# A fused attention and FFN kernel: casting loads on the GpSimd queue and a head pinned on TensorE

## The chip, the cores and the metric

The kernel runs on one core of a Trainium2 chip. The metric is the device time of one execution in microseconds (us). A run is called slow when its time is more than 1.5% above the fastest of the same kernel; such runs are left out of every comparison.

## The reference

Sliding-window causal attention is followed by a feed-forward network (FFN) with a squared ReLU, everything given and returned in fp32.

```python
# q, k, v: (8, 8, 576, 64)   batch, heads, tokens, head dimension
rel = pos[:, None] - pos[None, :]
mask = (rel >= 0) & (rel < 64)                      # window of 64
attn = softmax(where(mask, scale * q @ k.T, -1e9))
x = (attn @ v).transpose(0, 2, 1, 3).reshape(4608, 512)
h = maximum(x @ w_in, 0)                            # w_in  512 x 2048
out = (h * h) @ w_out                               # w_out 2048 x 512
```

The 4608 tokens are processed as 36 chunks of 128 tokens. Four chunks make one group of 512 for the FFN.

## The kernel before

All loads go out on the sync queue as fp32. DVE casts `w_in`, and GpSimd (POOL) casts `w_out`, q, k and v to fp16. Within a chunk each 64-token block attends to itself and to the block before it, so the values are kept twice: `v_ev` holds the chunk's own 128 rows, and `v_od` holds the same rows moved by 64. The lower half of `v_od` comes from the previous chunk. Both are rings of eight buffers.

```python
NV = 8
v_evs = [const.tile([P, H, 66], FP16, name=f"v_ev{i}") for i in range(NV)]
v_ods = [const.tile([P, H, 66], FP16, name=f"v_od{i}") for i in range(NV)]

def load(i):
    # ... k, q, v to fp32 staging tiles on the sync queue; GpSimd casts k and q ...
    v_ev, v_od, v_next = v_evs[i % NV], v_ods[i % NV], v_ods[(i + 1) % NV]
    nc.gpsimd.tensor_copy(out=v_ev[:, :, 0:D], in_=sts[2][:])
    nc.gpsimd.tensor_copy(out=v_od[64:P, :, 0:D], in_=v_ev[0:64, :, 0:D])
    if i + 1 < NCK:
        nc.gpsimd.tensor_copy(out=v_next[0:64, :, 0:D], in_=v_ev[64:P, :, 0:D])

def values(i):
    # ... for each head h and both 64-token blocks blk ...
    vv = (v_ods if blk == 0 else v_evs)[i % NV]
    nc.tensor.matmul(av[64 * blk:64 * blk + 64, h % 4, 0:65],
                     pms[i][h % 2][:, h // 2, blk, :], vv[:, h, 0:65], start=True, stop=True)
```

The head of the program treats the first eight chunks singly. T transposes q and k, S_ makes the scores, V multiplies by the values, and X transposes the result for the FFN. The `warm(n)` calls are matmuls without use that keep the clock of TensorE (PE) up. Below is the program order. The framework's scheduler may reorder it, but it respects every dependency that program order creates through a buffer.

```python
load(0)
for s in load_w_in(): s()
for i in range(1, NV - 1):
    load(i)
T(0), warm(6), S_(0), warm(6), V(0), warm(6), X(0), warm(4)
load(NV - 1)                       # chunk 7 is loaded AFTER V(0)
for s in load_w_out() + ffn_up_chunk(0): s()
T(1), S_(1), warm(2), V(1), T(2), warm(2), X(1), S_(2)
for i in range(1, NFIRST):
    up = ffn_up_chunk(i)
    up[0](), V(i + 1), T(i + 2), up[1](), up[2](), X(i + 1), S_(i + 2), up[3]()
# ... then groups: ffn_out(g-1), ffn_up(g), attention(g+1), loads(g+2), woven ...
```

The softmax here doesn't subtract the row's maximum and nothing guards it: scores larger than these inputs give would overflow.

## Time and profile before

| | before |
|---|---|
| median (4 runs) | 347.35 us (346.05 to 348.84) |
| profiled span | 345.9 us |
| PE busy | 324.3 us |

The page of the profile gives each engine's busy time. Below that are rows of 40 digits, each the busy share of one slice of 8.65 us in tenths. PEclk is the granted PE clock in tenths of full speed, and DMA is the mean busy share of the 16 DMA engines.

```profile
PE 324.3 (94%) x3146; PEld 178.2 (52%) x3146; DVE 207.9 (60%) x506; ACT 163.8 (47%) x289; POOL 121.5 (35%) x204
...
PE   1957888999999999999999999999999999999995
...
DVE  2656988852666776676776657665675566544400
...
PEclk9996999999999999999999999999999999999998
DMA  7799987899972455546877757730011000000021
```

PE is full from about the ninth slice on, so PE work bounds the kernel there. What can be gained lies in the first 75 us, and that is also where the DMA engines are near full. The table by stage of the same kernel gives, for each stretch, its length, the busy us of each engine (with instruction counts), the clock, the DMA share and GB/s.

```profile
core 0: us, PE busy (x) PEld busy (x) DVE busy (x) ACT busy (x) POOL busy (x), PEclk, DMA share, GB/s
0.00:20.00 20.00, 11.39 (x85) 5.24 (x86) 9.29 (x44) 2.97 (x4) 4.83 (x15) 1.00 0.76 222
20.00:75.00 55.00, 46.39 (x813) 40.10 (x811) 42.93 (x98) 29.01 (x52) 38.22 (x63) 0.94 0.94 240
75.00:100.00 25.00, 25.00 (x269) 13.71 (x267) 12.88 (x40) 10.28 (x19) 19.65 (x32) 1.00 0.89 214
100.00:346.00 246.00, 241.54 (x1989) 119.18 (x1987) 142.77 (x325) 121.51 (x215) 58.85 (x95) 1.00 0.37 96
```

From 20 to 75 us PE is busy 46.4 of 55 us, and DVE 42.9. After 75 us PE has no idle except the tail. Two more lines are wanted later. The first, from the timeline, is the first matmul of V(0), with its start and duration in us:

```profile
15.17 0.22 PE L211 MATMUL av<-v_od_121,pm_327 128*64 128x65 f16 x1 [0.26 <-DVE pm_327 L201]
```

The second is from the DMA issues of the first 8 us. It is the load of chunk 0's v, with its size and the us from issue to landing:

```profile
v_st<-in_v_dram SPq DMA_DIRECT2D x1, 256.0 KB, 3.9
```

V(0) starts at 15.2 us and waits only for its mask step on DVE.

### The profile page before, as it was taken

How to read it: one execution, taken by the hardware profiler on the slowest of the kernel's cores; microseconds unless marked ns; L12 is line 12 of the kernel's file. 1: busy time of each engine (PE TensorE's matmuls, PEld its weight loads, DVE VectorE, ACT ScalarE, POOL GpSimd, SP SyncE). 2: the span in 40 equal slices, each digit the busy share in tenths (PEclk: the TensorE clock that was granted, in tenths of full speed). 3: DMA queues.
4: the chain of work that ended last, by engine and by line, in shares of the span. 5: the costliest groups of instructions: out<-in, count | busy, mean ns of one | idle time of the engine just before them, and what ended most of it. 6: DMA issues, size and time to landing. Idle time of an engine off the chain costs nothing.

```text
span 345.9 us, 7917 instructions
## 1 busy us (share of the span) xinstructions
PE 324.3 (94%) x3146; PEld 178.2 (52%) x3146; DVE 207.9 (60%) x506; ACT 163.8 (47%) x289; POOL 121.5 (35%) x204
## 2 busy tenths in 40 slices
PE   1957888999999999999999999999999999999995
PEld 0346787875555555445545554455445544544442
DVE  2656988852666776676776657665675566544400
ACT  1123457544535646643664466436544654444411
POOL 4009895497753333316566544530000000000000
PEclk9996999999999999999999999999999999999998
DMA  7799987899972455546877757730011000000021
GB/s 200 249 252 239 234 247 252 207 230 228 243 172 61 93 121 123 121 124 155 212 185 182 170 135 184 185 87 27 23 45 36 30 32 32 30 30 32 35 88 62
DMA packets 122341, 46.65 MB, mean 135 GB/s; under 512 B 113600, under 2 KB 113600, under 8 KB 122304
## 3 DMA queue, kind: packets, MB, share of 16 engines
q1 hardware_dynamic: 122304, 46.15, 51.7%
q8 instruction: 24, 0.39, 0.5%
q14 instruction: 13, 0.11, 0.1%
HBM read 36.70 MB, written 9.44 MB: 133 GB/s over the span
## 4 chain that ended last, share of the span: by engine, by line
PE 83%; DVE 7%; DMA 5%; ACT 2%; SPq 1%; issue 1%; ACTq 0%
PE ops L296 37%; PE hps L250 28%; DMA ws<-in_moe_w_in_dram 5%; PE qkT_ps L173 4%; PE av L211 4%; PE xt_ps L224 2%; DVE h_397 L276 1%; DVE h_1087 L276 1%; DVE xT L226 1%; DVE w_in_sb L117 1%; PE hps_639 L271 1%; SPq L151 1%; SPq L115 0%; PE hps_1088 L271 0%; PE hps_1537 L271 0%
## 5 line engine op out<-in xcount | busy, mean ns | idle before, releaser
L250 PE MATMUL hps<-xT,w_in_sb 128*128 128x512 f16 x448 | 115.2, 379 | 0.0
L254 ACT ACTIVATE hrelu<-hps 128x512 f32<-128x512 f32 x112 | 66.8, 598 | 91.6 <-PE hps L250 90.9
L250 PEld LDWEIGHTS <-w_in_sb 128*128 128x128 f16 x448 | 43.7, 98 | 52.6 <-issue 0.3
L271 PEld LDWEIGHTS <-w_in_sb 128*128 128x128 f16 x512 | 31.2, 99 | 8.2 <-issue 3.9
L301 ACT ACTIVATE osb<-ops 128x512 f32<-128x512 f32 x36 | 21.6, 600 | 29.1 <-PE ops L296 28.9
L182 ACT ACTIVATE qT<-qkT_ps 128x512 f16<-128x512 f16 x36 | 21.5, 596 | 22.6 <-DVE kT L180 22.3
L216 DVE TENSOR_TENSOR x_sb<-av,rden 128x256 f16<-128x256 f32 x72 | 27.5, 415 | 0.1
L180 DVE COPY kT<-qkT_ps 128x512 f16<-128x512 f16 x36 | 15.2, 421 | 18.0 <-PE qkT_ps L173 17.8
L226 DVE COPY xT<-xt_ps 128x512 f16<-128x512 f16 x36 | 15.1, 420 | 12.7 <-PE xt_ps L224 12.7
L215 DVE RECIPROCAL rden<-av 128x4 f32<-128x4 f32 x72 | 11.4, 178 | 17.1 <-PE av L211 17.1
L255 DVE SCALAR_TENSOR_TENSOR h_5222<-hps,hrelu 128x512 f16<-128x512 f32 x16 | 11.1, 691 | 16.6 <-ACT hrelu L254 16.6
L296 PE MATMUL ops<-w_out_sb,h_1087 128*128 128x512 f16 x64 | 17.5, 380 | 0.0
L191 PEld LDWEIGHTS <-kT 64*128 64x128 f16 x576 | 11.0, 95 | 12.2 <-issue 9.6
L296 PE MATMUL ops<-w_out_sb,h_3120 128*128 128x512 f16 x64 | 16.5, 380 | 0.0
L296 PE MATMUL ops<-w_out_sb,h_2579 128*128 128x512 f16 x64 | 16.5, 380 | 0.0
L296 PE MATMUL ops<-w_out_sb,h_4199 128*128 128x512 f16 x64 | 16.5, 380 | 0.0
L296 PE MATMUL ops<-w_out_sb,h_3658 128*128 128x512 f16 x64 | 16.5, 380 | 0.0
L296 PE MATMUL ops<-w_out_sb,h_2041 128*128 128x512 f16 x64 | 16.5, 380 | 0.0
L296 PE MATMUL ops<-w_out_sb,h_4736 128*128 128x512 f16 x64 | 16.4, 379 | 0.0
L296 PE MATMUL ops<-w_out_sb,h_397 128*128 128x512 f16 x64 | 15.3, 380 | 0.0
L224 PE MATMUL xt_ps<-ident,x_sb 128*128 128x128 f16 x144 | 15.1, 222 | 0.1
L255 DVE SCALAR_TENSOR_TENSOR h_4736<-hps,hrelu 128x512 f16<-128x512 f32 x16 | 11.0, 689 | 6.8 <-ACT hrelu L254 6.4
(837 smaller groups left out, 611.1 us busy)
## 6 DMA issues: line engine op xcount, KB each, us to landing
out_dram<-osb SPq DMA_DIRECT2D x36, 256.0 KB, 2.2
k_st<-in_k_dram SPq DMA_DIRECT2D x32, 256.0 KB, 3.9
q_st<-in_q_dram SPq DMA_DIRECT2D x32, 256.0 KB, 4.0
v_st<-in_v_dram SPq DMA_DIRECT2D x32, 256.0 KB, 4.1
ws<-in_moe_w_in_dram SPq DMA_DIRECT2D x16, 256.0 KB, 4.2
k_st<-in_k_dram SPq DMA_DIRECT2D x8, 128.0 KB, 3.2
q_st<-in_q_dram SPq DMA_DIRECT2D x8, 128.0 KB, 3.0
v_st<-in_v_dram SPq DMA_DIRECT2D x8, 128.0 KB, 3.2
```

What stands on the lines that cost most here:

```text
L173: nc.tensor.transpose(out=ps[:, s, hp, :], in_=src[i][:, hp * P:(hp + 1) * P], identity=ident[:])
L180: nc.vector.tensor_copy(out=kT[:, :, 64:192], in_=ps[:, 0])
L182: nc.scalar.activation(out=qT[:], in_=ps[:, 1], func=AF.Copy, scale=1.0)
L216: nc.vector.tensor_tensor(out=x_sb[:, 4 * half:4 * half + 4, :], in0=av[:, :, 0:D], in1=rden[:].to_broadcast([P, 4, D]), op=ALU.mult)
L224: nc.tensor.transpose(out=xt[:, c, :], in_=xs[i][:, 2 * c:2 * c + 2, :], identity=ident[:])
L226: nc.vector.tensor_copy(out=xT_of(i // 4)[:, :, (i % 4) * P:(i % 4 + 1) * P], in_=xt[:])
L250: nc.tensor.matmul(hps[:], w_in_sb[:, c, f * P:(f + 1) * P], xT_of(g)[:, c, :], start=(c == 0), stop=(c == DMC - 1))
L254: nc.scalar.activation(out=hrelu[:], in_=hps[:], func=AF.Relu)
L255: nc.vector.scalar_tensor_tensor(out=h2s[g][:, f, :], in0=hps[:], scalar=0.0, in1=hrelu[:], op0=ALU.max, op1=ALU.mult)
L271: nc.tensor.matmul(hps[:, f, :], w_in_sb[:, c, (4 * fq + f) * P:(4 * fq + f + 1) * P], xT_of(g)[:, c, t0:t0 + P], start=(c == 0), stop=(c ...
L296: nc.tensor.matmul(hold["ps"][:], h2s[g][:, f, ts * P:(ts + 1) * P], w_out_sb[:, f, :], start=(f == 0), stop=(f == FFC - 1))
L301: nc.scalar.activation(out=osb[:], in_=hold["ps"][:], func=AF.Copy, scale=OUT_SCALE)
```

## The change

The intent is to free DVE and POOL from casts and to feed PE earlier. Every load but chunk 0's becomes a casting transfer on the GpSimd queue, straight to fp16. The weights come in quarters of 1 MB (read) placed between the chunks. The shifted copies of v become transfers from SBUF to SBUF on the sync queue. PE's order for the first eight chunks is written out by hand, chunk by quarter of the FFN, and pinned. Cut to its core:

```diff
+    def shift_v(i):
+        v_ev, v_od, v_next = v_evs[i % NV], v_ods[i % NV], v_ods[(i + 1) % NV]
+        nc.sync.dma_start(out=v_od[64:P, :, 0:D], in_=v_ev[0:64, :, 0:D])
+        if i + 1 < NCK:
+            nc.sync.dma_start(out=v_next[0:64, :, 0:D], in_=v_ev[64:P, :, 0:D])
+
+    def load(i):
+        # ... for k, q, v:
+                nc.gpsimd.dma_start(out=dst[p0:p1, :, 0:D], in_=src[b, :, t0:t0 + p1 - p0, :]...)
+        shift_v(i)
+    # load_first(): chunk 0 as before in fp32 on the sync queue, cast on DVE and ACT
+    # load_w_in(quar), load_w_out(quar): one casting gpsimd transfer each
...
+    load_first()
+    load_w_in(0)
+    load_w_in(1)
     # ... masks ...
-    load(0)
-    for s in load_w_in():
-        s()
-    for i in range(1, NV - 1):
+    load(1)
+    load_w_in(2)
+    load(2)
+    load_w_in(3)
+    for i in range(3, NV):
         load(i)
-    T(0), warm(6), S_(0), warm(6), V(0), warm(6), X(0), warm(4)
-    load(NV - 1)
-    for s in load_w_out() + ffn_up_chunk(0):
-        s()
-    T(1), S_(1), warm(2), V(1), T(2), warm(2), X(1), S_(2)
-    for i in range(1, NFIRST):
-        ...
+    for quar in range(4):
+        load_w_out(quar)
+    with tc.manual_schedule(engines={mybir.EngineType.PE}):
+        T(0), warm(4), S_(0), warm(4), V(0), warm(4), X(0), warm(2)
+        up_chunk(0, 0), warm(4), up_chunk(0, 1), warm(4)
+        T(1), S_(1), warm(2), V(1), warm(2), X(1), up_chunk(1, 0)
+        up_chunk(0, 2), up_chunk(1, 1), up_chunk(1, 2), T(2), S_(2), up_chunk(0, 3), V(2)
+        up_chunk(1, 3), X(2), T(3), up_chunk(2, 0), S_(3), up_chunk(2, 1)
+        for i in range(2, NFIRST):
+            # V(i+1), up(i,2), X(i+1), T(i+2), up(i,3), S_(i+2), up(i+1,0), up(i+1,1)
```

More of the change, by code (lines that the diff above doesn't have):

```diff
@@ L45 @@
     NB = S // 64
-    W_SCALE = 100.0
-    OUT_SCALE = 1.0 / (W_SCALE * W_SCALE)
+    H_SCALE = 1.0e4
+    OUT_SCALE = 1.0 / H_SCALE
     BIG = 65504.0
@@ L53 @@
     const = ctx.enter_context(tc.tile_pool(name="const", bufs=1))
-    wst = ctx.enter_context(tc.tile_pool(name="wst", bufs=4))
-    stage = ctx.enter_context(tc.tile_pool(name="stage", bufs=15))
+    stage = ctx.enter_context(tc.tile_pool(name="stage", bufs=3))
     st16 = ctx.enter_context(tc.tile_pool(name="st16", bufs=8))
@@ L65 @@
     ps_att = ctx.enter_context(tc.tile_pool(name="ps_att", bufs=4, space=bass.MemoryType.PSUM))
+    NV = 8
+    FQ = DFF // 4
+    NFIRST = 8
     ident = const.tile([P, P], FP16, name="ident")
+    base = const.tile([P, 64], FP16, name="base")
+    w_in_q = [const.tile([P, DMC, FQ], FP16, name=f"w_in{i}") for i in range(4)]
+    w_out_q = [const.tile([P, 4, DM], FP16, name=f"w_out{i}") for i in range(4)]
+    v_evs = [const.tile([P, H, 66], FP16, name=f"v_ev{i}") for i in range(NV)]
+    v_ods = [const.tile([P, H, 66], FP16, name=f"v_od{i}") for i in range(NV)]
@@ new lines, with pieces @@
+    k16s, q16s = {}, {}
+    def pieces(i):
+        b0, j0 = divmod(2 * i, NB)
+        if j0 + 1 < NB:
+            return [(0, P, b0, 64 * j0)]
+        return [(0, 64, b0, 64 * j0), (64, P, b0 + 1, 0)]
+    def shift_v(i):
[4 more added lines that the diff above has]
+    def load(i):
+        k16s[i] = st16.tile([P, H, D], FP16, name="k16", tag="k16")
+        q16s[i] = st16.tile([P, H, D], FP16, name="q16", tag="q16")
+        for (src, dst) in ((k, k16s[i]), (q, q16s[i]), (v, v_evs[i % NV])):
+            for (p0, p1, b, t0) in pieces(i):
+                nc.gpsimd.dma_start(
+                    out=dst[p0:p1, :, 0:D],
+                    in_=src[b, :, t0:t0 + p1 - p0, :].rearrange("h p d -> p h d"))
+        shift_v(i)
@@ new lines, in load_first @@
+    def load_first():
+        k16s[0] = st16.tile([P, H, D], FP16, name="k16", tag="k16")
+        q16s[0] = st16.tile([P, H, D], FP16, name="q16", tag="q16")
+        for (src, dst, cast) in ((k, k16s[0], nc.vector.tensor_copy),
+                                 (q, q16s[0], nc.scalar.copy),
+                                 (v, v_evs[0], nc.vector.tensor_copy)):
+            st = stage.tile([P, H, D], FP32, name="first_st", tag="st")
+            nc.sync.dma_start(out=st[:], in_=src[0, :, 0:P, :].rearrange("h p d -> p h d"))
+            cast(out=dst[:, :, 0:D], in_=st[:])
+        shift_v(0)
@@ new lines, in load_w_in, with load_w_out @@
+    def load_w_in(quar):
+        nc.gpsimd.dma_start(
+            out=w_in_q[quar][:],
+            in_=moe_w_in[:, quar * FQ:(quar + 1) * FQ].rearrange("(c p) n -> p c n", p=P))
+    def load_w_out(quar):
+        nc.gpsimd.dma_start(
+            out=w_out_q[quar][:],
+            in_=moe_w_out[4 * quar * P:4 * (quar + 1) * P, :].rearrange("(f p) n -> p f n", p=P))
+    for i in range(NV):
+        nc.vector.memset(v_evs[i][:, :, 64:65], 1.0)
+        nc.vector.memset(v_ods[i][:, :, 64:65], 1.0)
@@ L68 @@
+    nc.vector.memset(v_ods[0][0:64, :, 0:D], 0.0)
     make_identity(nc, ident[:])
-    base = const.tile([P, 64], FP16, name="base")
+    load_first()
+    load_w_in(0)
+    load_w_in(1)
     nc.gpsimd.memset(base[:], BIG)
@@ L96 @@
     mask_second = make_mask("mask_second", 1)
-    w_in_sb = const.tile([P, DMC, DFF], FP16, name="w_in_sb")
-    w_out_sb = const.tile([P, FFC, DM], FP16, name="w_out_sb")
-    NV = 8
-    v_evs = [const.tile([P, H, 66], FP16, name=f"v_ev{i}") for i in range(NV)]
-    v_ods = [const.tile([P, H, 66], FP16, name=f"v_od{i}") for i in range(NV)]
-    for i in range(NV):
-        nc.vector.memset(v_evs[i][:, :, 64:65], 1.0)
-        nc.vector.memset(v_ods[i][:, :, 64:65], 1.0)
-    nc.vector.memset(v_ods[0][0:64, :, 0:D], 0.0)
-    def load_w_in():
-        steps = []
-        FQ = DFF // 4
-        def one(quar, c):
-            ws = wst.tile([P, FQ], FP32, name="ws", tag="ws")
-            nc.sync.dma_start(out=ws[:], in_=moe_w_in[c * P:(c + 1) * P,
-                                                      quar * FQ:(quar + 1) * FQ])
-            nc.vector.tensor_scalar(
-                out=w_in_sb[:, c, quar * FQ:(quar + 1) * FQ], in0=ws[:],
-                scalar1=W_SCALE, scalar2=None, op0=ALU.mult)
-        for quar in range(4):
-            for c in range(DMC):
-                steps.append(lambda quar=quar, c=c: one(quar, c))
-        return steps
-    def load_w_out():
-        def one(f):
-            ws = wst.tile([P, DM], FP32, name="ws2", tag="ws")
-            nc.sync.dma_start(out=ws[:], in_=moe_w_out[f * P:(f + 1) * P, :])
-            nc.gpsimd.tensor_copy(out=w_out_sb[:, f, :], in_=ws[:])
-        return [lambda f=f: one(f) for f in range(FFC)]
     xTs = {}
@@ L140, in xT_of @@
         return xTs[g]
-    q16s, k16s, qTs, kTs, pms, xs = {}, {}, {}, {}, {}, {}
-    def load(i):
-        sts = []
-        for (src, nm) in ((k, "k"), (q, "q"), (v, "v")):
-            st = stage.tile([P, H, D], FP32, name=f"{nm}_st", tag="st")
-            b0, j0 = divmod(2 * i, NB)
-            if j0 + 1 < NB:
-                nc.sync.dma_start(
-                    out=st[:], in_=src[b0, :, 64 * j0:64 * j0 + P, :].rearrange("h p d -> p h d"))
-            else:
-                nc.sync.dma_start(
-                    out=st[0:64], in_=src[b0, :, 64 * j0:S, :].rearrange("h p d -> p h d"))
-                nc.sync.dma_start(
-                    out=st[64:P], in_=src[b0 + 1, :, 0:64, :].rearrange("h p d -> p h d"))
-            sts.append(st)
-        k16s[i] = st16.tile([P, H * D], FP16, name="k16", tag="k16")
-        nc.gpsimd.tensor_copy(out=k16s[i][:], in_=sts[0][:].rearrange("p h d -> p (h d)"))
-        q16s[i] = st16.tile([P, H * D], FP16, name="q16", tag="q16")
-        nc.gpsimd.tensor_copy(out=q16s[i][:], in_=sts[1][:].rearrange("p h d -> p (h d)"))
-        v_ev, v_od, v_next = v_evs[i % NV], v_ods[i % NV], v_ods[(i + 1) % NV]
-        nc.gpsimd.tensor_copy(out=v_ev[:, :, 0:D], in_=sts[2][:])
-        nc.gpsimd.tensor_copy(out=v_od[64:P, :, 0:D], in_=v_ev[0:64, :, 0:D])
-        if i + 1 < NCK:
-            nc.gpsimd.tensor_copy(out=v_next[0:64, :, 0:D], in_=v_ev[64:P, :, 0:D])
+    qTs, kTs, pms, xs = {}, {}, {}, {}
     def transposes(i):
@@ L172, in transposes @@
             for hp in range(HP):
-                nc.tensor.transpose(out=ps[:, s, hp, :], in_=src[i][:, hp * P:(hp + 1) * P],
+                nc.tensor.transpose(out=ps[:, s, hp, :], in_=src[i][:, 2 * hp:2 * hp + 2, :],
                                     identity=ident[:])
@@ L242, with h2_of, square @@
     h2s = {}
+    def h2_of(g):
+        if g not in h2s:
+            h2s[g] = h2pool.tile([P, FFC, 512], FP16, name="h2", tag="h2")
+        return h2s[g]
+    def square(out, hps, hrelu):
+        nc.scalar.activation(out=hrelu, in_=hps, func=AF.Relu, scale=H_SCALE)
+        nc.vector.scalar_tensor_tensor(
+            out=out, in0=hps, scalar=0.0, in1=hrelu, op0=ALU.max, op1=ALU.mult)
     def ffn_up(g):
-        h2s[g] = h2pool.tile([P, FFC, 512], FP16, name="h2", tag="h2")
         def one(f):
@@ L250, in one, with up_chunk @@
                 nc.tensor.matmul(
-                    hps[:], w_in_sb[:, c, f * P:(f + 1) * P], xT_of(g)[:, c, :],
+                    hps[:], w_in_q[f // 4][:, c, f % 4 * P:(f % 4 + 1) * P], xT_of(g)[:, c, :],
                     start=(c == 0), stop=(c == DMC - 1))
             hrelu = hrp.tile([P, 512], FP32, name="hrelu", tag="hrelu")
-            nc.scalar.activation(out=hrelu[:], in_=hps[:], func=AF.Relu)
-            nc.vector.scalar_tensor_tensor(
-                out=h2s[g][:, f, :], in0=hps[:], scalar=0.0, in1=hrelu[:],
-                op0=ALU.max, op1=ALU.mult)
+            square(h2_of(g)[:, f, :], hps[:], hrelu[:])
         return [lambda f=f: one(f) for f in range(FFC)]
-    def ffn_up_chunk(i):
+    def up_chunk(i, fq):
         g, t0 = i // 4, i % 4 * P
-        if g not in h2s:
-            h2s[g] = h2pool.tile([P, FFC, 512], FP16, name="h2", tag="h2")
-        def one(fq):
-            hps = ps_up.tile([P, 4, P], FP32, name="hps4", tag="ps_u")
-            for f in range(4):
-                for c in range(DMC):
-                    nc.tensor.matmul(
-                        hps[:, f, :], w_in_sb[:, c, (4 * fq + f) * P:(4 * fq + f + 1) * P],
-                        xT_of(g)[:, c, t0:t0 + P], start=(c == 0), stop=(c == DMC - 1))
-            hrelu = hrp.tile([P, 4, P], FP32, name="hrelu4", tag="hrelu")
-            nc.scalar.activation(out=hrelu[:], in_=hps[:], func=AF.Relu)
-            nc.vector.scalar_tensor_tensor(
-                out=h2s[g][:, 4 * fq:4 * fq + 4, t0:t0 + P], in0=hps[:], scalar=0.0,
-                in1=hrelu[:], op0=ALU.max, op1=ALU.mult)
-        return [lambda fq=fq: one(fq) for fq in range(FFC // 4)]
+        hps = ps_up.tile([P, 4, P], FP32, name="hps4", tag="ps_u")
+        for f in range(4):
+            for c in range(DMC):
+                nc.tensor.matmul(
+                    hps[:, f, :], w_in_q[fq][:, c, f * P:(f + 1) * P],
+                    xT_of(g)[:, c, t0:t0 + P], start=(c == 0), stop=(c == DMC - 1))
+        hrelu = hrp.tile([P, 4, P], FP32, name="hrelu4", tag="hrelu")
+        square(h2_of(g)[:, 4 * fq:4 * fq + 4, t0:t0 + P], hps[:], hrelu[:])
     def warm(n):
@@ L294, in one @@
                 hold["ps"] = ps_out.tile([P, DM], FP32, name="ops", tag="ps_o")
-            for f in range(4 * fq, 4 * fq + 4):
+            for f in range(4):
                 nc.tensor.matmul(
-                    hold["ps"][:], h2s[g][:, f, ts * P:(ts + 1) * P], w_out_sb[:, f, :],
-                    start=(f == 0), stop=(f == FFC - 1))
+                    hold["ps"][:], h2s[g][:, 4 * fq + f, ts * P:(ts + 1) * P], w_out_q[fq][:, f, :],
+                    start=(fq == 0 and f == 0), stop=(fq == 3 and f == 3))
             if fq == 3:
@@ L306, in ffn_out @@
         return [lambda ts=ts, fq=fq: one(ts, fq) for ts in range(4) for fq in range(4)]
-    load(0)
-    for s in load_w_in():
-        s()
-    NFIRST = 8
-    for i in range(1, NV - 1):
-        load(i)
-    T, S_, V, X = [lambda i, fn=fn: fn(i) if i < NFIRST else None
-                   for fn in (transposes, scores, values, to_xT)]
-    T(0), warm(6), S_(0), warm(6), V(0), warm(6), X(0), warm(4)
-    load(NV - 1)
-    for s in load_w_out() + ffn_up_chunk(0):
-        s()
-    T(1), S_(1), warm(2), V(1), T(2), warm(2), X(1), S_(2)
-    for i in range(1, NFIRST):
-        up = ffn_up_chunk(i)
-        up[0](), V(i + 1), T(i + 2), up[1](), up[2](), X(i + 1), S_(i + 2), up[3]()
+    load(1)
[3 more added lines that the diff above has]
+    for i in range(3, NV):
+        load(i)
+    for quar in range(4):
+        load_w_out(quar)
+    with tc.manual_schedule(engines={mybir.EngineType.PE}):
+        T, S_, V, X = transposes, scores, values, to_xT
+        T(0), warm(4), S_(0), warm(4), V(0), warm(4), X(0), warm(2)
[4 more added lines that the diff above has]
+        for i in range(2, NFIRST):
+            steps = [lambda: V(i + 1), lambda: up_chunk(i, 2), lambda: X(i + 1),
+                     lambda: T(i + 2), lambda: up_chunk(i, 3), lambda: S_(i + 2),
+                     lambda: up_chunk(i + 1, 0), lambda: up_chunk(i + 1, 1)]
+            live = [i + 1 < NFIRST, True, i + 1 < NFIRST, i + 2 < NFIRST, True,
+                    i + 2 < NFIRST, i + 1 < NFIRST, i + 1 < NFIRST]
+            for step, on in zip(steps, live):
+                if on:
+                    step()
     for s in loads(2):
```

## The prediction

> **What bounds the kernel now.** TensorE. The page has PE busy 324.3 of 345.9 us. From 86.5 us to its end at about 341.6 us the table by stage shows no idle. The matmul counts confirm it: FFN matmuls of 512 columns stream at 0.213 us, 16 of 128 columns at 0.9 us, one chunk's attention at about 1.75 us. All of the program's useful matmuls then sum to about 310 us (448 up + 576 out x 0.213, 512 small up x 0.056, 36 x 1.75), an estimate. So 310 us are PE work, 4.3 tail, some 31 lost in the first 70 us. There the DMA engines are 70 to 106% busy at 200 to 270 GB/s (table of slices), DVE is at 83 to 96% between 34 and 69 us, and the granted clock falls to 0.5 between 26 and 32 us.
>
> **What the change removes and adds.** Removed: 16 weight casts on DVE (0.43 us each, 7 us) and every POOL cast (0.61 us each, 121.5 us busy in all). POOL was never the bound, so that is worth nothing after 70 us. DVE relief is worth a few us in the head. Added: three descriptor-generating DMAs per chunk on POOL, and two SBUF-to-SBUF shifts per chunk on the sync queue. The matmul count is unchanged. If PE ran its new head unhindered from about 20 us, the kernel would end near 335 us.
>
> **Why I expect no such gain.** The compiled instruction order shows that pinning the eight chunks does not keep other matmuls out: the scheduler has put first output-projection matmuls, which need the first and second quarter of w_out, before chunk 1's last transposes and before chunk 1's first up-projection. PE runs in order, so it stops there, with only about 5.5 us of useful work done, until two w_out quarters have landed. On the load queue these are behind all of w_in and chunks 1 to 7: 12.6 MB in all.
> The bytes are unchanged, and in the head the DMA engines are already near full. The Trainium skill, "DMA: Bandwidth & Descriptors", section "Issuing engines are not separate DMA queues", says that transfers run on the same 16 engines whichever engine starts them; so I expect no more bandwidth from the GpSimd queue. Estimates from this trace: 256 KB of q, k or v per 1.1 us (19 in 22.5 us), so 23.5 us for seven chunks; weights at about 350 GB/s (366 GB/s at 12 to 14 us), 18 us for 6 MB; chunk 0 and start 6 us; shifts 3 to 4 us. The second w_out quarter lands at about 51 us.
> After that PE is fed: 51 + 304.5 of remaining work + 4.3 tail + 2.5 for a cold clock after the stall = 362 us.
>
> **Prediction:** 362 us, 8 in 10 between 350 and 388. Faster by over 2%: 0.06; within 2%: 0.14; slower by over 2%: 0.80.
>
> **What would show it.** Right: a PE gap of 20 to 35 us ending at 45 to 60 us, released by a w_out transfer, ahead of a two-matmul output group; the clock at 0.5 around its end; PE full afterwards; DVE free of weight casts; DMA near full until the gap ends. Wrong: PE busy through 20 to 50 us, or gaps released by chunk loads or DVE.
>
> **What would make it wrong.** Casting transfers moving faster than the 240 GB/s seen here (w_out by 35 us would make it even, below that faster). Descriptor generation on POOL slower than about 1.1 us per 256 KB transfer: the stall grows one for one, and above about 2.5 us the loads would bound the later stages too, giving 390 us or more.

## The result

| | before | after |
|---|---|---|
| median | 347.35 us (346.05 to 348.84, 4 runs) | 380.74 us (379.83 to 381.78, 4 runs) |
| profiled span | 345.9 us | 378.0 us |
| PE busy | 324.3 us | 322.9 us |
| ratio to before, 95% interval | 1 | 1.0956 (1.0919 to 1.0993) |

A ratio, here and below, is the one that the record gives for the fast runs of two kernels measured in the same rounds, with its 95% interval. It isn't quite the ratio of the medians quoted. The change makes the kernel 33.4 us slower. The prediction was slower by 14.6.

The page of the profile after:

```profile
PE 322.9 (85%) x3146; PEld 177.4 (47%) x3146; DVE 196.3 (52%) x492; ACT 164.6 (44%) x290; POOL 105.5 (28%) x134
...
PE   1400047999999999999999999999999999999996
...
DVE  1300014477878765756665665666566665744310
...
PEclk9965558999999999999999999999999999999999
DMA  8999995599999999799779959996110000001012
```

There is a hole in PE from the third to the fifth slice, with the clock down to half. From the eighth slice PE is full. The table by stage of the kernel after, first two stretches:

```profile
0.00:20.00 20.00, 5.44 (x32) 2.08 (x32) 4.69 (x29) 3.58 (x5) 13.54 (x24) 1.00 1.37 162
20.00:75.00 55.00, 20.15 (x233) 13.55 (x233) 9.62 (x23) 6.82 (x12) 20.97 (x26) 0.66 1.31 121
```

In the 55 us from 20 to 75, PE does 20.2 us of work against 46.4 before. That one stretch loses 26.2 us, and the first 20 us lose 6.0, together 32.2. PE's busy time as a whole is nearly unchanged and the spans differ by 32.1, so the whole loss is in the head. (DMA shares above 1 mean that packets overlap on an engine.)

What PE waited for, from the view of waits (columns: engine, tile and line, releaser, then total us, times, longest us):

```profile
PE av L207 <- DMA v_od<-v_ev: 33.9, 1, 33.9
PE warm L279 <- DVE mask_inner L145: 8.7, 1, 8.7
PE qkT_ps L169 <- DVE k L111: 4.6, 1, 4.6
```

One wait of 33.9 us stands out. The prediction named a `w_out` transfer as its releaser, and "gaps released by chunk loads or DVE" as the sign of being wrong. The releaser is part of a chunk load: the shift of the values, `v_od<-v_ev`. The timeline shows where it ends:

```profile
52.77 0.21 PE L207 MATMUL av<-v_od,pm 128*64 128x65 f16 x1 [33.88 <-DMA v_od<-v_ev]
```

This is the first matmul of V(0), which had started at 15.2 us before. The chain of waits from 34 us to there (start, us, what ran):

```profile
33.87 0.81 POOL q L97
34.68 6.81 DMA v_ev<-in_v_dram
...
41.50 0.59 SPq L87
...
42.15 10.58 DMA v_od<-v_ev
52.73 0.04 issue
52.77 0.65 PE av L207 x13
```

The transfer at 34.68 us is the v of chunk **7**. When it lands, the sync queue issues chunk 7's shift, which takes 10.58 us, and only then does PE start the values of chunk **0**. Two lines of the DMA issues tell how busy the engines were (the first v of chunk 0 on the sync queue, and the four `w_out` quarters; size written and median us to landing):

```profile
first_st<-in_v_dram SPq DMA_DIRECT2D x1, 256.0 KB, 11.2
...
w_out<-in_moe_w_out_dram POOLq DMA_DIRECT2D x4, 512.0 KB, 11.3
```

### The profile page after: what moved, and what is told of

Same layout as the page of the kernel before. It is cut to its first block, busy times and chain, and to the rows that moved or that the text cites. A ratio compares the mean times of both kernels' runs of the same rounds, so it can differ in the third digit from the quotient of the medians.

```text
span 378.0 us, 7791 instructions
## 1 busy us (share of the span) xinstructions
PE 322.9 (85%) x3146; PEld 177.4 (47%) x3146; DVE 196.3 (52%) x492; ACT 164.6 (44%) x290; POOL 105.5 (28%) x134
## 3 DMA queue, kind: packets, MB, share of 16 engines
HBM read 36.70 MB, written 9.44 MB: 122 GB/s over the span
## 4 chain that ended last, share of the span: by engine, by line
PE 76%; DMA 10%; ACT 5%; DVE 4%; POOL 3%; issue 1%; SPq 0%; ACTq 0%; POOLq 0%
PE ops L289 33%; PE hps L255 26%; DMA w_in<-in_moe_w_in_dram 6%; PE hps L269 5%; PE av L207 4%; PE qkT_ps L169 3%; PE sc L187 3%; DMA v_od<-v_ev 3%; ACT hrelu L246 3%; DVE h L247 2%; PE xt_ps L220 2%; DMA v_ev<-in_v_dram 2%; ACT pm L195 1%; PE warm L279 1%; POOL v_ev L97 1%
## 5 line engine op out<-in xcount | busy, mean ns | idle before, releaser
L289 PE MATMUL ops<-w_out,h 128*128 128x512 f16 x576 | 149.9, 382 | 0.0
L247 DVE SCALAR_TENSOR_TENSOR h<-hps,hrelu 128x512 f16<-128x512 f32 x144 | 99.3, 690 | 65.5 <-ACT hrelu L246 63.0
L255 PE MATMUL hps<-xT,w_in 128*128 128x512 f16 x448 | 115.0, 379 | 0.0
L289 PEld LDWEIGHTS <-h 128*128 128x128 f16 x576 | 49.7, 98 | 41.9 <-issue 0.6
L255 PEld LDWEIGHTS <-w_in 128*128 128x128 f16 x448 | 43.8, 98 | 52.9
L97 POOL DMA_DIRECT2D v_ev<-in_v_dram x39 | 32.8, 841 | 90.1 <-PE av L207 86.1
L97 POOL DMA_DIRECT2D k<-in_k_dram x39 | 33.0, 847 | 58.5 <-PE qkT_ps L169 55.9
L207 PE MATMUL av<-v_od,pm 128*64 128x65 f16 x288 | 17.6, 200 | 35.0 <-DMA v_od<-v_ev 33.9
L195 ACT ACTIVATE pm<-sc 128x512 f16<-128x512 f32 x72 | 39.2, 599 | 4.5 <-PE sc L187 4.5
L207 PEld LDWEIGHTS <-pm 128*64 128x64 f16 x576 | 13.1, 112 | 50.0 <-issue 44.9
L269 PE MATMUL hps<-xT,w_in 128*128 128x128 f16 x512 | 33.0, 220 | 1.2 <-DVE h L247 0.9
L97 POOL DMA_DIRECT2D q<-in_q_dram x39 | 33.0, 847 | 3.0 <-DMA q<-in_q_dram 1.6
L269 PEld LDWEIGHTS <-w_in 128*128 128x128 f16 x512 | 29.9, 98 | 3.8 <-issue 2.3
L176 DVE COPY kT<-qkT_ps 128x512 f16<-128x512 f16 x36 | 15.2, 423 | 18.9 <-PE qkT_ps L169 18.8
L222 DVE COPY xT<-xt_ps 128x512 f16<-128x512 f16 x36 | 15.2, 422 | 16.5 <-PE xt_ps L220 16.4
## 6 DMA issues: line engine op xcount, KB each, us to landing
w_in<-in_moe_w_in_dram POOLq DMA_DIRECT2D x4, 512.0 KB, 10.8
```

The costliest lines, as they stand in the source:

```text
L97: nc.gpsimd.dma_start(out=dst[p0:p1, :, 0:D], in_=src[b, :, t0:t0 + p1 - p0, :].rearrange("h p d -> p h d"))
L195: nc.scalar.activation(out=pm[:], in_=sc[hh][:], func=AF.Exp, scale=1.0 / float(D) ** 0.5)
L207: nc.tensor.matmul(av[64 * blk:64 * blk + 64, h % 4, 0:65], pms[i][h % 2][:, h // 2, blk, :], vv[:, h, 0:65], start=True, stop=True)
L247: nc.vector.scalar_tensor_tensor(out=out, in0=hps, scalar=0.0, in1=hrelu, op0=ALU.max, op1=ALU.mult)
L255: nc.tensor.matmul(hps[:], w_in_q[f // 4][:, c, f % 4 * P:(f % 4 + 1) * P], xT_of(g)[:, c, :], start=(c == 0), stop=(c == DMC - 1))
L269: nc.tensor.matmul(hps[:, f, :], w_in_q[fq][:, c, f * P:(f + 1) * P], xT_of(g)[:, c, t0:t0 + P], start=(c == 0), stop=(c == DMC - 1))
```

## Theories

Why should chunk 0 wait for chunk 7? `shift_v(7)` writes the lower half of `v_next = v_ods[(7 + 1) % 8]`, which is `v_ods[0]`, for chunk 8. The changed program issues `load(7)` before V(0), and V(0) reads `v_ods[0]` whole. In program order this is a write followed by a read of the same buffer, so the framework makes V(0) wait. The data isn't needed: chunk 0's mask zeroes the weights of those rows, so the output is right either way. The kernel before called `load(7)` after V(0), and so had no such wait. The compiled order of the changed kernel, with what each instruction waits for, shows it (a listing of the compiled program, not a view of the profile). Below are the first values of chunk 0 on PE, the last shift on the sync queue before it, and the first output matmuls on PE, each with its row in that engine's order:

```
PE  65 L207 Ldweights pm0_261 [waits DMAHW3_49,DVE_49]
PE  66 L207 Matmult av_273<-v_od0_109,pm0_261 64x65 [waits DMAHW2_49]
...
SP  18 L87 DMACopy v_od7_116<-v_ev7_108 64x8x64 [waits DMAHW1_49,DMASW3_49]
SP  19 L89 DMACopy v_od0_109<-v_ev7_108 64x8x64 [waits DMAHW2_49]
...
PE 285 L289 Ldweights h2_330 [waits DMASW4_49]
PE 286 L289 Matmult ops_1497<-w_out0_97,h2_330 128x512 [waits PE_49]
...
PE 302 L289 Matmult ops_1497<-w_out1_98,h2_330 128x512 [waits DMASW5_49]
```

The sync queue's transfers take the semaphores DMAHW0 to 7 in turn, and row 19, chunk 7's shift into `v_od0`, has DMAHW2 (as rows 3 and 11 had before it; in a rebuild of the kernel the wait is for the third of these, so for row 19). The values of chunk 0 wait for DMAHW2 at row 66. The output matmuls that wait for the first and second quarter of `w_out` come 220 rows later.

- **A, the ring:** the 34 us are this false dependency. It is made by eight buffers together with loading chunk 7 before V(0). Ending it should bring back nearly all of the 33 us.
- **W, the prediction's account:** the time is lost because output matmuls, moved forward in PE's fixed order, need `w_out`, which lands last. The ring's wait would only stand in front of it, and without the ring PE would stall there instead.
- **L, a rival:** the loads are merely slow in the casting queue, and chunk 0's own shift lands late. Then ending the ring's dependency changes little.

A second question: without any stall, is the new head worth anything (the prediction: about 335 us)?

## Experiments

Twelve kernels were run, all with correct outputs. Each expectation below names its theories as it goes.

| kernel | what | median us | ratio to before [95%] |
|---|---|---|---|
| e1_ring9 | after, `v_od` ring of nine | 353.25 | 1.0139 [1.0093, 1.0184] |
| e9_load7_late | after, chunk 7 loaded behind V(0) | 351.88 | 1.0124 [1.0089, 1.0158] |
| e2_pinall | after, the whole program pinned on PE | 388.13 | 1.1125 [1.1076, 1.1174] |
| e3_ring9_pinall | e1 and e2 together | 356.86 | 1.025 [1.0207, 1.0292] |
| e12_pinall_wout_late | e2, `w_out` held back | 380.72 | 1.0928 [1.0874, 1.0981] |
| e4_ring9_hoist | e3, early output matmuls by hand | 369.98 | 1.0626 [1.0578, 1.0673] |
| e5_ring9_nopin | e1, nothing pinned | 351.79 | 1.01 [1.0068, 1.0132] |
| e6_before_pinned | before, with the pinned head | 351.84 | 1.0109 [1.0065, 1.0153] |
| e7_ring9_quiet | e1, quiet start tried | 355.84 | 1.0213 [1.0169, 1.0258] |
| e8_ring9_quiet_nopin | e7, nothing pinned | 348.06 (3 fast runs) | 1.0007 [0.9965, 1.0049] |
| e10_quiet_forced | e5, quiet start forced | 349.08 | 1.0043 [1.0, 1.0087] |
| e11_quiet_poolshift | e10, shifts as GpSimd copies | 356.25 | 1.0248 [1.0205, 1.0291] |

The median of the kernel before in the same rounds was 348.55 us (e1 to e4), 348.14 (e5 to e8), 348.06 (e9 to e11) and 348.23 (e12), seven runs each.

### e1_ring9: nine buffers in the shifted ring

```diff
-    v_ods = [... for i in range(NV)]
+    NVO = NV + 1
+    v_ods = [... for i in range(NVO)]
-        v_ev, v_od, v_next = v_evs[i % NV], v_ods[i % NV], v_ods[(i + 1) % NV]
+        v_ev, v_od, v_next = v_evs[i % NV], v_ods[i % NVO], v_ods[(i + 1) % NVO]
-                    vv = (v_ods if blk == 0 else v_evs)[i % NV]
+                    vv = v_ods[i % NVO] if blk == 0 else v_evs[i % NV]
```

> One edit: the v_od ring gets nine buffers in place of eight, so that chunk 7's second shift no longer writes the buffer that chunk 0's value matmuls read; the scheduler is left free and now puts its first early output matmul behind chunk 2's values instead of behind chunk 1's. Theory A (the changed kernel's stall is chunk 0's values waiting for chunk 7's shift, a dependency that only the ring and the order of the program make): chunk 0's values run before 25 us, PE next stops at the early output matmul for the first w_out quarter until about 44 us, time 342 to 358 us. Rival L (loads are merely slow in the casting queue, chunk 0's own shift lands late): chunk 0's values still wait to about 50 us and the time stays at 375 to 381 us.

Measured: 353.25 us, 27.5 less than after. The waits of PE in e1:

```profile
PE ops L291 <- DMA w_out<-in_moe_w_out_dram: 3.5, 1, 3.5
PE av L209 <- DMA v_od<-v_ev: 3.1, 1, 3.1
```

V(0) now waits 3.1 us for its own shift and runs at 22.2 us, so L falls. The wait that the prediction had named, output matmuls on `w_out`, is there, but it is 3.5 us long. One extra buffer took away most of the loss, as A says. It changed a second thing, though. The scheduler now puts the first output matmuls later: they stood between chunk 1's values and X(1) in after, and stand among chunk 2's values in e1 (46.4 us in its timeline). So e1 alone doesn't tell A from W.

### e9_load7_late: the same dependency ended by program order

```diff
-    for i in range(3, NV):
+    for i in range(3, NV - 1):
         load(i)
...
         T(0), warm(4), S_(0), warm(4), V(0), warm(4), X(0), warm(2)
+        load(NV - 1)
```

> The changed kernel with eight ring buffers and its pinned order; only chunk 7's load is written behind chunk 0's values, where the kernel before has it. It takes the dependency of chunk 0's values away by other means than e1. Theory A: chunk 0's values run before 22 us, time like e1 (353 us, between 346 and 362). If e1's gain came from the ninth buffer itself and not from this dependency: 375 us or more.

Measured: 351.88 us, with the ring still of eight. The timeline of e9, the first matmul of V(0):

```profile
22.31 0.21 PE L207 MATMUL av<-v_od,pm 128*64 128x65 f16 x1 [3.12 <-DMA v_od<-v_ev]
...
41.76 0.81 PE L289 MATMUL ops<-w_out,h 128*128 128x512 f16 x3 [1.73 <-DMA w_out<-in_moe_w_out_dram]
```

V(0) runs at 22.3 us instead of 52.8. Two different ways of ending the dependency bring nearly the same, 27.5 and 28.9 us. That excludes that the extra buffer helped by some other way, such as its place in memory. But in e9 too the scheduler moved the first output matmuls back (the second line: behind T(2), where in after they stood before X(1)), and they wait only 1.7 us. The next runs hold the order fixed, and these tell A from W.

### e2_pinall and e3_ring9_pinall: no output matmul can come forward

In both, all that follows the head stands in the pinned block as well, so that no output matmul can be moved ahead of it. e3 has the ring of nine as well.

```diff
     with tc.manual_schedule(engines={mybir.EngineType.PE}):
         # ... head ...
-    for s in loads(2):
-        s()
-    for g in range(1, NTB + 1):
-        ...
+        for s in loads(2):
+            s()
+        for g in range(1, NTB + 1):
+            ...
```

> One edit: the rest of the program is pinned on TensorE too, so that no output matmul comes before chunk 7's last up-projection; the ring stays at eight. Theory W (the recorded prediction: output matmuls hoisted ahead of their weights make the stall): gap gone, time at most 345 us. Theory A: the gap stays from about 20 to 53 us, released by a v shift, and the time is 372 to 384 us.

> Both edits: nine ring buffers and everything pinned. Theory A with W as a second, hidden stall: no PE wait over 6 us after 20 us, first 70 us better packed than before, time 330 to 342 us, faster than before by 2 to 5 per cent. Rival L: PE still waits for loads between 20 and 50 us for more than 15 us in all, time 360 us or more.

Measured: 388.13 us for e2 and 356.86 us for e3. The wait in e2:

```profile
PE av L207 <- DMA v_od<-v_ev: 34.1, 1, 34.1
```

With no output matmul ahead of it, the stall is as long as in after (34.1 us against 33.9). So the moved matmuls don't make it, and W falls as the cause. The ring alone, from e2 to e3, is worth 31.3 us. e2 came out a little above what was expected (372 to 384). Behind the stall, from 60 to 125 us, its PE waits 10.3 us for ACT and DVE, against 3.1 in after, where output matmuls stand in between. e3 missed by far: 330 to 342 us were expected of a head without stalls. This opened the second question.

### e12_pinall_wout_late: why the shift took 10.6 us

In after, chunk 7's shift of 64 KB took 10.58 us while `w_out` was landing beside it. Here a small copy that reads the shifted rows and writes each `w_out` quarter holds the `w_out` transfers back until the shift has landed.

```diff
     for quar in range(4):
+        nc.gpsimd.tensor_copy(out=w_out_q[quar][:, 0, 0:D], in_=v_ods[0][:, 0, 0:D])
         load_w_out(quar)
```

> e2 (eight buffers, everything pinned, so the stall of the changed kernel on chunk 0's values alone) with the four w_out transfers held back until chunk 7's shift has landed, by a small GpSimd copy that reads the shifted buffer. In the changed kernel that shift was issued at 42.1 us and landed 10.6 us later with 4 MB of w_out in flight beside it. If that traffic is what makes the shift so long: it lands in 3 to 5 us, chunk 0's values start at 44 to 48 us, and the time falls by 4 to 9 us against e2's 388 to 379 to 384 us. If the shift is slow by itself: chunk 0's values at 50 us or later and a time within 2 us of e2.

Measured: 380.72 us, 7.4 less than e2. The chain of waits in e12:

```profile
41.99 2.39 DMA v_od<-v_ev
44.39 0.04 issue
44.43 0.65 PE av L207 x16
```

The same shift takes 2.39 us when 4 MB of `w_out` aren't in flight, and V(0) starts at 44.4 us. So of the 34 us stall, about 8 come from a small transfer on the sync queue that shares the DMA engines with bulk casting transfers. Most of the rest is chunk 7's place behind the other loads: in the chain of after two `w_in` quarters follow each other until 25.1 us, then GpSimd issues the transfers of the later chunks one behind the other until 34.7, and then the v of chunk 7 takes 6.8 us.

### e4_ring9_hoist: the stall that was predicted, made on purpose

e3 with the first group's output matmuls put by hand into the head, about where the scheduler had moved them in after.

```diff
+        F = ffn_out(0)
-        T(1), S_(1), warm(2), V(1), warm(2), X(1), up_chunk(1, 0)
+        T(1), S_(1), warm(2), V(1), warm(2), F[0](), X(1), F[1](), up_chunk(1, 0)
         # ... F[2](), F[3]() behind T(2) and up_chunk(1, 3), then two per chunk ...
-            streams = [(ffn_out(g - 1), 0.0, 1.0)]
+            streams = [(ffn_out(g - 1), 0.0, 1.0)] if g > 1 else []
```

> Nine ring buffers, everything pinned, but the output matmuls of the first token group written by hand at the early places that the changed kernel's compiled order has: four of the first w_out quarter before chunk 1's last transposes, four of the second before chunk 1's first up-projection. This is the prediction's stall alone. Theory W as hidden second stall: PE stops there until the second w_out quarter lands at 45 to 49 us, released by a w_out transfer, time 354 to 368 us, against e3's 330 to 342 us. If the hoist were harmless: within 3 us of e3.

Measured: 369.98 us, 13.1 more than e3 and a little over the 354 to 368 expected. The timeline of e4:

```profile
31.71 1.04 PE L281 MATMUL warm<-mask_inner,ident 128*128 128x512 f16 x2
...
44.24 1.89 PE L291 MATMUL ops<-w_out,h 128*128 128x512 f16 x4 [11.50 <-DMA w_out<-in_moe_w_out_dram]
...
47.00 1.43 PE L291 MATMUL ops<-w_out,h 128*128 128x512 f16 x4 [0.44 <-DMA w_out<-in_moe_w_out_dram]
```

PE stands for 11.5 us until the first quarter has landed, and 0.4 more for the second. So the mechanism of the prediction exists in such an order, and its end (47.0 us for the second quarter, against 51 predicted) was close. In after it couldn't act: PE reached those matmuls only at 65.1 us, and the four quarters had landed between 43.9 and 52.1. So W is not the cause in after, but it was right about what stood behind it. With the output matmuls this early (and the rest pinned as well), ending the ring's wait leaves 370 us, only 10.8 less than after. The larger gains of e1 and e9 need the later place that the scheduler then found for them.

### e5_ring9_nopin and e6_before_pinned: loads and order apart

e5 is e1 with the order of PE left to the scheduler. e6 is the kernel before, with its own loads and casts, but with the pinned head (`load(7)` and the `w_out` loads stay behind V(0)).

```diff
 # e5, against e1
-    with tc.manual_schedule(engines={mybir.EngineType.PE}):
+    if True:
 # e6, against before
+    with tc.manual_schedule(engines={mybir.EngineType.PE}):
-    T(0), warm(6), S_(0), warm(6), V(0), warm(6), X(0), warm(4)
-    load(NV - 1)
-    ...
+        T(0), warm(4), S_(0), warm(4), V(0), warm(4), X(0), warm(2)
+        load(NV - 1)
+        for s in load_w_out(): s()
+        up_chunk(0, 0), warm(4), up_chunk(0, 1), warm(4)
+        # ... as in the change
```

> As e1 with nine ring buffers, but the first eight chunks are not pinned on TensorE: the scheduler orders everything. It tells what pinning costs or gives beside casting loads. If the fixed order of chunk by quarter is what spends the time that e1 (353 us) shows over the ideal: 340 to 349 us. If pinning is neutral: within 3 us of e1. If it helps: 356 us or more.

> The kernel before, its loads and casts untouched, with the changed kernel's pinned order of the first eight chunks (loading of chunk 7 stays behind chunk 0's values, as it is in the kernel before). It is the other half of the change alone. If pinning costs by itself: 350 to 362 us; if it is neutral: 345 to 350 us.

Measured: 351.79 and 351.84 us. With e1 and e9 this makes a table of two by two, ratios to before:

| | PE order free | PE order pinned |
|---|---|---|
| loads as before | 1 | 1.0109 (e6) |
| casting loads, no ring dependency | 1.0100 (e5) | 1.0139 (e1), 1.0124 (e9) |

Either half alone costs about 1%, and together they cost 1.2 to 1.4%; all four are within the 2% that counts as the same, and the intervals of e5, e1 and e9 overlap. So neither is the gain that the change was made for. Of e5's alternatives the neutral one came true (within 3 us of e1), not the gain (340 to 349 us); for e6 it was the cost (350 to 362 us). The halves aren't quite pure: e5 keeps the new program order as the scheduler's input, and the new start of chunk 0.

Two lines show where each half pays. The first is the wait of the scores for qT on ScalarE (ACT), whole run, before:

```profile
PE sc_1342 L191 <- ACT qT L182: 0.4, 1, 0.4
...
PE sc_893 L191 <- ACT qT L182: 0.3, 1, 0.3
...
PE sc_2382 L191 <- ACT qT L182: 0.2, 1, 0.2
```

and in e6:

```profile
PE sc L191 <- ACT qT L182: 5.9, 6, 1.4
```

The order by hand puts the scores of a chunk so close behind its transposes that PE waits for the copy of qT, 5.9 us in six waits against 0.9 before. The program order before has two quarters of the FFN and an X between them, the order by hand one quarter. The second is the start of DVE in e1 (timeline):

```profile
3.90 0.67 DVE L112 CAST k<-first_st 128x512 f16<-128x512 f32 x1 [1.99 <-DMA first_st<-in_k_dram]
13.83 0.43 DVE L112 CAST v_ev<-first_st 128x512 f16<-128x512 f32 x1 [9.26 <-DMA first_st<-in_v_dram]
14.17 0.42 DVE L178 COPY kT<-qkT_ps 128x512 f16<-128x512 f16 x1
```

DVE also runs in order. The cast of chunk 0's v stands ahead of the copy of kT that chunk 0's scores need, and of the masks. The v took 11.9 us to land in e1, so DVE stood for 9.3 us and everything of chunk 0 began late: the first up-projection at 25.6 us, against 19.4 before.

### e7_ring9_quiet, e8_ring9_quiet_nopin, e10_quiet_forced: a quiet start

In after the v of chunk 0 took 11.2 us to land, against 3.9 before, beside two `w_in` quarters issued at the same time. These three kernels try to hold the casting transfers back until chunk 0 has landed. e7 does it by program order, with chunk 0 cast and shifted on GpSimd, and e8 is the same with nothing pinned. e10 is e8 with a dependency that forces it.

```diff
 # e7, against e1
-        for (src, dst, cast) in ((k, k16s[0], nc.vector.tensor_copy), ...):
+        for (src, dst) in ((k, k16s[0]), (q, q16s[0]), (v, v_evs[0])):
             ...
-            cast(out=dst[:, :, 0:D], in_=st[:])
-        shift_v(0)
+            nc.gpsimd.tensor_copy(out=dst[:, :, 0:D], in_=st[:])
+        nc.gpsimd.tensor_copy(out=v_ods[0][64:P, :, 0:D], in_=v_evs[0][0:64, :, 0:D])
+        nc.gpsimd.tensor_copy(out=v_ods[1][0:64, :, 0:D], in_=v_evs[0][64:P, :, 0:D])
     # and load_first(), load_w_in(0), load_w_in(1) stand behind the mask base
 # e10, against e8
+    for i in range(2):
+        nc.gpsimd.tensor_copy(out=w_in_q[i][:, 0, 0:D], in_=v_evs[0][:, 0, 0:D])
     load_w_in(0)
     load_w_in(1)
```

> As e1, but the start is the one of before: chunk 0 is cast and shifted by GpSimd from the staging buffers, the mask base is built first, and the first casting weight transfer is issued only behind these. In the changed kernel chunk 0's v took 11.2 us to land beside two 1 MB casting transfers, 4 us before, and chunk 0's shift 5 us more. If that traffic delays the start: v lands within 5 us, chunk 0's values run by 15 us in place of 19.7, time 3 to 7 us under e1 (346 to 350 us). If not: within 2 us of e1.

> Both of e5 and e7: quiet start, nothing pinned, nine buffers. If both gains hold and add: 336 to 345 us, faster than the kernel before. If the casting loads give nothing even so: 346 us or more.

> e5 (nine buffers, nothing pinned) with the quiet start made certain: a small GpSimd write into the first two w_in quarters, which reads chunk 0's cast v, stands ahead of their transfers, so that no casting weight transfer is under way while chunk 0 lands (e7 and e8 did not achieve this; there one was issued at 1.4 us and v landed at 10.4). If the casting transfers slow chunk 0: v lands within 5.5 us of its issue, chunk 0's values run by 12.5 us, and the time is 2 to 7 us under e5 (345 to 350 us). If they don't: v lands as late as 9 us or more.

Measured: e7 355.84 us, 2.6 more than e1 and outside both its alternatives, and e8 348.06 us (its "346 us or more"). As tests of a quiet start both failed as built: the scheduler still issued one `w_in` quarter at 1.4 us, and in e7 chunk 0's v took 8.4 us and landed at 10.4. In e7's fixed order PE then waits 8.1 us for chunk 1's shift, until 29.0 us, and 6.0 us for `w_out`. One of e8's four runs, the profiled one, took 549.51 us at a mean granted clock of 0.562; the other three lay between 347.84 and 349.58 us and are what its median and ratio are made of.

Even so e8 shows something. It differs from e5 only in the start, chunk 0 cast and shifted on GpSimd and the `w_in` loads issued later, and it is level with before (1.0007) where e5 is not (1.0100, measured in the same rounds, intervals apart). So the loss of e5 sits in its start; which part of that edit mends it was not separated.

e10 did what it was built for. Its DMA issues, then its waits:

```profile
first_st<-in_v_dram SPq DMA_DIRECT2D x1, 256.0 KB, 5.4
```

```profile
PE hps L272 <- DMA w_in<-in_moe_w_in_dram: 5.7, 2, 5.0
```

Chunk 0's v lands in 5.4 us and V(0) starts at 10.9 us, 11 us earlier than in e1. But then the first up-projection waits 5.0 us for the `w_in` that was held back, and the kernel ends at 349.08 us, 2.7 under e5 as expected. That is level with before: the interval of its ratio, 1.0 to 1.0087, leaves a cost of nothing up to 0.9%. The forcing can't claim these 2.7 us, since e8 has the same edits without it and is no slower.

### e11_quiet_poolshift: the shifts off the DMA engines

```diff
-        nc.sync.dma_start(out=v_od[64:P, :, 0:D], in_=v_ev[0:64, :, 0:D])
+        nc.gpsimd.tensor_copy(out=v_od[64:P, :, 0:D], in_=v_ev[0:64, :, 0:D])
 # and the same for v_next
```

> e10 with the shifts of v as GpSimd copies of 0.61 us, as before has them, in place of transfers that took 3.5 us at the median and up to 10.6 us. If the transfers' time to land is what holds early chunks back: no wait of TensorE for a shift over 1 us, time 2 to 6 us under e10, perhaps 340 to 346 us, faster than before. If not: within 2 us of e10, or slower because GpSimd now waits for v before it issues later loads.

Measured: 356.25 us, 7.2 more than e10. The wait that came up in e11:

```profile
PE ops L292 <- DMA w_out<-in_moe_w_out_dram: 7.2, 1, 7.2
```

GpSimd issues in order. With a copy behind each chunk's loads it waits for that chunk's v to land before it can issue the next loads, up to 6.9 us at a time, and `w_out` is issued at 50.3 to 54.9 us instead of 39.9 to 42.5. The expectation had named this outcome. Whether the shifts on the sync queue hold the head back stays open, as the edit brought a larger cost of its own.

## Where the prediction was wrong

The direction, the place and the shape of the loss were right: a hole in PE of 20 to 35 us (33.9 measured) that ends at 45 to 60 us (52.8), a clock at 0.5 around it, PE full afterwards, DVE free of weight casts. The cause given for it was not, and the time was off by 18.7 us, more than the whole predicted loss of 14.6.

**The step that failed.** "PE runs in order, so it stops there, with only about 5.5 us of useful work done, until two w_out quarters have landed." PE stopped earlier, at the values of chunk 0 with about 1 us of useful work done, and waited 33.9 us there for chunk 7's shift, because of the ring of eight and because chunk 7 was loaded first (e2 against e3; e1, e9). The output matmuls waited for nothing in after: they first ran at 65.1 us, when `w_out` had landed. For the prediction the compiled order was read for which matmul stands where, but not for what each one waits for; the wait of V(0) on a shift stood in it. That the stall ended near the 51 us forecast (52.8) is chance. The two waits hang on neighbouring transfers in one load queue, the v of chunk 7 with its shift and the first half of `w_out`; made on purpose, the forecast one ended at 47.0 us (e4).

**What the sum got wrong, term by term** (profiled span; the last column is measured less predicted):

| term | predicted us | measured us | difference |
|---|---|---|---|
| stall ends | 51 | 52.8 | +1.8 |
| useful PE work left then | 304.5 | about 309 | +4.5 |
| warm-up matmuls after the stall (estimate) | 0 | about 6.2 | +6.2 |
| cold clock and short waits after it | 2.5 | about 6.2 (the rest) | +3.7 |
| tail behind the last matmul | 4.3 | 3.8 | −0.5 |
| sum | 362.3 | 378.0 | +15.7 |

The largest terms follow from the stop's true place. Stopping at V(0), PE had done only chunk 0's transposes and scores, about 1 us, and 18 of the 26 warm-up matmuls still stood behind the stall, where they cost time instead of filling it. The first six of them ran at about half clock, at 0.43 us each or a little more. "Useful work" and "the rest" are worked out with the prediction's own durations and by subtraction, so these two are not independent. The median of the runs lies another 2.7 us above the profiled span.

**"If PE ran its new head unhindered from about 20 us, the kernel would end near 335 us."** No run without the ring's wait came near: 356.9 (e3), 353.3 (e1), 351.9 (e9), 351.8 (e5), 349.1 (e10), 348.1 (e8, fast runs). The gain expected of casting loads has three holes that the runs show. Chunk 0 lands later beside the bulk transfers (11.2 us against 3.9), so DVE, in order, holds back the start of chunk 0 (e1). When the start is cleared, `w_in` comes later (e10). And the pinned order costs about 1% by itself, with the old loads (e6, where the waits for qT grew by 5.0 us); beside casting loads no cost of pinning clear of noise was seen (e1 against e5). What the residual 1.0% of e5 is made of was not isolated, beyond that a changed start takes it away (e8).

**Points that held.** The bytes read from HBM are unchanged (36.70 MB on both pages), and so is PE's work (322.9 us busy against 324.3). GpSimd's descriptor work did not bound the later stages. The group of q, k and v transfers on POOL in after, with busy us and mean ns of one:

```profile
L97 POOL DMA_DIRECT2D k<-in_k_dram x39 | 33.0, 847 | 58.5 <-PE qkT_ps L169 55.9
```

At 0.85 us per transfer this stays below the 1.1 us that the prediction named as a limit. In the head, though, it lies on the chain: from 25.4 to 34.7 us POOL is busy 8.3 of 9.3 us with issuing, and chunk 7's v comes last. One remark in it was too pessimistic: "no more bandwidth from the GpSimd queue". Eight chunks and all weights, 14.7 MB read, had landed by about 52 us in after, an estimate of 282 GB/s from the last landing in the trace; before moved 222 and 240 GB/s in its first two stages. (The GB/s column of after is lower because it counts the fp16 bytes written.) It helped nothing, since PE was waiting for one small copy at the end of that queue.

**What the Trainium skill gave.** "DMA: Bandwidth & Descriptors", section "Issuing engines are not separate DMA queues", says that transfers from every issuing engine interleave on the same 16 engines. The traces fit that for both transfers that were measured with and without bulk traffic from the other queue: 2.39 against 10.58 us for a shift of 64 KB (e12 and after), and 5.4 against 11.2 us for chunk 0's v (e10, with no weights in flight, and after). The same page, section "Anatomy of one DMA — SWDGE (gpsimd) path", says that a semaphore wait happens on the issuing sequencer and not in the DMA engine. The chain of after agrees: the sync queue issued the shift at 41.5 to 42.1 us, right behind the landing of chunk 7's v at 41.5. "TensorE: Matmul & The Clock Gate", section "What's actually happening", says that an idle PE falls to 4/8 of its clock. The PEclk row of after shows 5 through the hole.

## What to carry to other kernels

When loads are moved ahead, check which buffers of a ring they wrap into: with a ring of N, loading N items before the first use makes the first consumer wait for the last load if any load also writes its neighbour's buffer, and one more buffer, or that one load behind the first use, ends it. Before predicting from a compiled order, read for each early instruction of an in-order engine what it waits for, not only where it stands. A small copy that is turned into a transfer took 2.4 us here on a quiet DMA and 10.6 beside bulk loads, so it should not be put on the chain that starts the kernel. When an edit removes one wait, check whether the scheduler has moved other work as well, and hold the order fixed in one of the runs.

## What the Trainium skill lacked or had wrong

- "DMA: Bandwidth & Descriptors", section "Anatomy of one DMA — SWDGE (gpsimd) path", calls descriptor generation "small, variable", with no figure in that row. Here it kept POOL busy for 0.85 us per q, k or v transfer (1024 rows of 256 bytes read) and 0.83 us per weight quarter of 1 MB, so it was nearly the same for both.
- The same page has no figure for what a small transfer pays beside bulk casting transfers. Here: 64 KB from SBUF to SBUF in 2.39 us quiet and 10.58 us busy, and 256 KB of chunk 0 in 5.4 (e10) and 11.2 us.
- "TensorE: Matmul & The Clock Gate" tells of clock records stuck at a quarter for over 50 us. One run of e8, on one core, had a mean granted clock of 0.562 over its 549.5 us (0.54 to 0.56 in every stage from 20 us on), while the three other runs of the same kernel were near 0.98. Nothing here shows why.
- The cause of the loss is not a matter for these pages: the wait of 33.9 us was made by a ring of buffers and program order, not by the chip.
